# Head of a sort-attention and gated-MLP kernel: v loaded behind a memset, products of zeros between balancing steps, the first k sort in one-bank pieces

## The chip, the cores and the metric

One core of one Trainium2 chip. The metric is the device time of one execution in microseconds (us), as the median of several runs. Five engines work on it: TensorE (PE in the profile, its weight loads PEld), VectorE (DVE), ScalarE (ACT), GpSimd (POOL) and SyncE (SP); each runs its own list of instructions in order and waits on semaphores.

## What is computed

Attention over blocks whose keys and values are first mixed by a balanced matrix, then a two-layer network with the gate h cos h. Cut to what matters:

```
P = sort_net                                  # (4, 8, 8, 8)
for _ in range(5):                            # balancing
    P = exp(P - max(P)); P = P / (sum over columns + 1e-9); P = P / (sum over rows + 1e-9)
k_sorted = einsum('bhij,bhjcd->bhicd', P, k_blocks)     # 8 blocks of 96 rows, 64 wide
v_sorted = einsum('bhij,bhjcd->bhicd', P, v_blocks)
scores = q_block @ k_sorted_block.T / 8; attn = softmax(scores)
x = (attn @ v_sorted), reshaped to (3072, 512)
h = x @ w_in;  out = (h * cos(h)) @ w_out     # 512 -> 2048 -> 512
```

## The kernel before

The order on every engine is written out by hand. The work goes in eight units n (batch b = n // 2, half of the blocks), each with 4 block rows u. Per unit: `qk` (L368) makes scores of one block row in PSUM and subtracts the row maxima on DVE; `expo` (L379) takes the exponential on ACT; the result is turned by `p_transpose` (L392) on PE or by a DMA; `av` (L399) multiplies with v and divides on DVE; `x_transpose` (L428) turns the result into `xT`. `moe_up` (L477) then makes eight `h` tiles with cos on ACT and the product on DVE, and `moe_down` (L482) the output. Attention of unit n + 1 is put in slots between the pieces of `moe_up` and `moe_down` of unit n, so only the head, before the first `moe_up`, has attention alone.

The head, L141 to L529. POOL makes the identity, clears the padding of four `p_buf` tiles (L146), then issues the loads in this order: q of unit 0 (L148, instruction at L114), k of batch 0 in two halves (L149, L94), v of batch 0 in two halves (L150, L94), three quarters of `w_in` (L152, L135). Then it clears the rows of `vbuf` between v's halves (L154, L155), writes ones into `vS` (L159), and issues the last quarter of `w_in`, q of unit 1, `w_out`, k of batch 1 and q of unit 2 (L161 to L166). Later loads stand behind these in the same queue.

Meanwhile the balancing runs (L197 to L283), for two groups g of two batches each: one small product on PE (`sk`, L217) and a few DVE and ACT instructions per step. `keep_warm` (L179) puts products of a zero tile, 128x128 by 128x256, ahead of it (16) and behind its first two steps (6 and 6); nothing reads them. q of unit 0 is turned on PE in two of the steps (`q_turn`, L245). At the end `spread` (L233) writes the balanced matrix of each group into `bd` as a block diagonal.

`k_sort_b` (L284) applies it to k: for each column c of a block and each half of the heads, one product with 32 rows of `kbuf` as weights and 32 columns of `bd`. It takes 32 columns c per call, so a tile `ks` of two PSUM banks; the left half of the result is copied to `kT` by DVE, the right half by ACT (L291 to L298). Three calls make batch 0. `v_sort_b` (L325) does the same for v, eight products of 128x128 by 64 per call, copied by ACT to `vS`; eight such calls (`v_next`) stand between the first scores (L498 to L513).

PSUM has two pools: `big` (three buffers of two banks: `idle`, `ks`, `sc`, `av`, `h`) and `acc` (two buffers of one bank: `sk`, `vs`, `pps`, `xps`, `o`). A buffer is taken in turn, and its next writer waits for the readers of the last.

Of the kernel before, what the change touches and what calls it, by code (L numbers as in the profile page):

```python
# [10 lines left out]
FP32 = mybir.dt.float32  # L11
BF16 = mybir.dt.bfloat16
# [6 lines left out]
def kernel(  # L19
# [15 lines left out]
    nc = tc.nc  # L35
    B, H, S, D = q.shape
    nb = sort_net.shape[-1]
# [7 lines left out]
    H2 = H // 2  # L45
# [63 lines left out]
    def load_q(n):  # L109
        b, ih = n // 2, n % 2  # L110
        if n < NQ:

            t = qload.tile([blk, H, QR * D], BF16, name="qin", tag="qin")
            nc.gpsimd.dma_start(  # L114
                out=t[:], in_=q[b][:, ih * IC * blk:(ih + 1) * IC * blk].rearrange(
                    "h (p r) d -> p h (r d)", r=QR))
# [16 lines left out]
    def load_w_in(z):  # L133
        c = slice(z * Dff // 4, (z + 1) * Dff // 4)
        nc.gpsimd.dma_start(out=w_in_t[:, :, c], in_=w_in_d[:, :, c])  # L135
# [3 lines left out]
        nc.gpsimd.dma_start(out=w_out_t[:, c], in_=w_out_d[:, c])  # L139

    make_identity(nc, ident[:])  # L141
    NP = 4
    p_bufs = []
    for i in range(NP):
        t = const.tile([blk, 2 * H2, 128], BF16, name=f"p_buf{i}")
        nc.gpsimd.memset(t[:, :, blk:], 0.0)  # L146
        p_bufs.append(t)
    load_q(0)  # L148
    load(kbuf, kin_d, 0)  # L149
    load(vbuf, vin_d, 0)  # L150
    for z in range(3):
        load_w_in(z)  # L152

    nc.gpsimd.memset(vbuf[32:64, :CD], 0.0)  # L154
    nc.gpsimd.memset(vbuf[96:128, :CD], 0.0)  # L155
    VW = D + 2
    for g in range(NG):
        vS[g] = vsp.tile([blk, 4 * NB, VW], BF16, name="vS", tag="vS")
        nc.gpsimd.memset(vS[g][:, :, D:D + 1], 1.0)  # L159
        kT[g] = ktp.tile([128, 2 * NB, blk], BF16, name="kT", tag="kT")  # L160
    load_w_in(3)  # L161
    load_q(1)
    for z in range(4):
# [4 lines left out]
    order = const.tile([blk, blk], BF16, name="order")  # L168
    half_pi = const.tile([128, 1], FP32, name="half_pi")
    nc.vector.memset(half_pi[:], math.pi / 2)  # L170
    warm = const.tile([128, 256], BF16, name="warm")
    nc.vector.memset(warm[:], 0.0)
    nc.vector.memset(vbuf[:, CD:], 0.0)
    nc.vector.memset(vperm[:, CD:], 0.0)
# [3 lines left out]

    def keep_warm(times):  # L179

        idle = big.tile([128, 256], FP32, name="idle", tag="big")
        for _ in range(times):
            nc.tensor.matmul(idle[:], warm[:, :128], warm[:], start=True, stop=True)

    keep_warm(16)


    E = [const.tile([128, nb], FP32, name=f"E{g}") for g in range(NG)]
# [34 lines left out]
        nc.vector.scalar_tensor_tensor(  # L223
            L[g][:], rows_of, ci[g][:], along(E[g]), op0=ALU.mult, op1=ALU.mult)
    sk = [product(L[g], maskj) for g in range(NG)]
    keep_warm(6)
    nc.vector.tensor_copy(same[:], rows_of)
    for g in range(NG):
        nc.vector.tensor_scalar(
# [34 lines left out]
    for it in range(4):  # L264
        for g in range(NG):
            nc.scalar.activation(E[g][:], T[g][:], AF.Exp, scale=ci[g][:])
        if it > 1:
            copy_on(A, *turned)
        sk = [product(same, E[g]) for g in range(NG)]
        if it in (1, 2):  # L270
            turned = q_turn(0, it - 1, big, "big")
        elif it == 0:
            keep_warm(6)
        for g in range(NG):
            nc.vector.reciprocal(rr[g][:], sk[g][:])
            nc.vector.tensor_tensor_reduce(
                T[g][:], E[g][:], rr[g][:], 1.0, 1e-9, ALU.mult, ALU.add, cs[g][:])
            nc.vector.reciprocal(ci[g][:], cs[g][:])
            if it == 3:
                spread(g)  # L280

    def k_sort_b(b, c0, ncs, eng, pool, tag):

        ps = pool.tile([128, ncs, NB], FP32, name="ks", tag=tag)  # L284
        for t in range(ncs):
            c = c0 + t
            for hp in range(2):
                r = hp * 64 + b * 32
                x = hp * H + b * H2
                nc.tensor.matmul(  # L290
                    ps[hp * D:(hp + 1) * D, t], kbuf[r:r + 32, c * D:(c + 1) * D],  # L291
                    bds[0][r:r + 32, x:x + H2].rearrange("p x i -> p (x i)"),
                    start=True, stop=True)
        engs = eng if isinstance(eng, list) else [eng]
        w = NB // len(engs)
        for z, e in enumerate(engs):
            copy_on(e, kT[0][:, b * NB + z * w:b * NB + (z + 1) * w, c0:c0 + ncs],
                    ps[:, :, z * w:(z + 1) * w].rearrange("p t m -> p m t"))  # L298

    def k_sort_g(c0, ncs, eng, pool, tag):  # L300
        ps = pool.tile([128, ncs, 2 * NB], FP32, name="ks", tag=tag)
# [48 lines left out]
    def qk_part(n, u, part, pool, tag):  # L350
        g, b2, ih = where(n)
        w = len(part)
        sc = pool.tile([128, w, 512], FP32, name="sc", tag=tag)
        for e, hp in enumerate(part):
            for h2 in range(H2):
                m = (b2 * H2 + h2) * nb + ih * IC + u
                nc.tensor.matmul(  # L357
                    sc[:blk, e, h2 * blk:(h2 + 1) * blk],
                    qT[n][hp * D:(hp + 1) * D, u * H2 + h2, :],
                    kT[g][hp * D:(hp + 1) * D, m, :], start=True, stop=True)  # L360
# [126 lines left out]
    B, C = (big, "big"), (acc, "acc")  # L487


    vz = iter(range(16))  # L490

    def v_next(eng=A):
        z = next(vz)
        v_sort_b(z // 8, z % 8 * 8, 8, eng, *C)
# [9 lines left out]
    expo(0, 0, True)  # L504
    qk(0, 2)
    v_next()
    p_transpose(0, 0, A, *C)
    v_next()
    expo(0, 1, True)
    qk(0, 3)  # L510
    v_next()
    v_next()
    p_transpose(0, 1, V, *C)  # L513
# [18 lines left out]
    expo(1, 0, True)  # L532
    expo(1, 1, True)
    moe_down(0, [[(qk, 1, 2), (p_transpose, 1, 0, A, *B)],
                 [(k_sort_b, 1, 0, 32, [V, A], *B), (p_transpose, 1, 1, A, *B), (qk, 1, 3),
                  (expo, 1, 2, True)],
                 [(av, 1, 0, True), (av, 1, 1, True), (expo, 1, 3, True),
                  (p_transpose, 1, 2, A, *B)],
                 [(k_sort_b, 1, 32, 32, [V, A], *B), (x_transpose, 1, 0, V, *B),
                  (av, 1, 2, True), (p_transpose, 1, 3, A, *B)],  # L540
                 [(k_sort_b, 1, 64, 32, [V, A], *B), (av, 1, 3, True),
                  (x_transpose, 1, 1, V, *B)],
                 [(q_transpose, 2, 0, A, *B), (x_transpose, 1, 2, V, *B),
                  (x_transpose, 1, 3, V, *B)]])
# [119 lines left out]
```

## Time and profile before

| what | us |
|---|---|
| runs: median (lowest to highest of 3) | 276.68 (275.47 to 276.81) |
| profiled execution, whole | 278.54 |
| profiled execution, span | 276.8 |
| PE busy in the span | 249.6 (90%) |
| DVE, ACT, POOL busy | 171.0, 158.6, 95.4 |
| k of batch 0: issue begins, first k product | 3.24, 15.21 |
| bd of group 0 written | 12.98 |
| first score product, first up product | 23.49, 36.77 |

The page gives busy times by engine, the span in 40 slices of 6.92 us with PE's granted clock and the DMA engines' share, the chain of work that ended last, the costliest groups of instructions, and the DMA issues. Besides the page, the trace answers with the chain in order of time, busy times in chosen stretches, and the DMA queues in a stretch. A busy PE isn't PE at its peak: matmul ends are modelled, and at half clock the same product is longer.

### The profile page before, as it was taken

Reading aid. Unit: us, or ns where it says so; the run is one execution under the profiler, and the core shown is the slowest. Engines: PE = TensorE matmul, PEld = TensorE weight load, DVE = VectorE, ACT = ScalarE, POOL = GpSimd, SP = SyncE. Lnnn points to the kernel's source line nnn. Section 1 sums busy time; section 2 is a strip of 40 time slices with the busy share of each in tenths; the row PEclk is TensorE's granted clock in tenths of the full one; section 3 lists DMA queues with packets and bytes.
Section 4 is the critical chain, followed back from the end, with each engine's and each line's share of the span. In section 5 each row is a group of like instructions: output and inputs, shape, how many; then the busy total and the mean of one; then the engine's idle time right before and its main releaser. Section 6 shows DMA issues by size and latency. Waiting matters only on the chain.

```text
span 276.8 us, 6148 instructions
## 1 busy us (share of the span) xinstructions
PE 249.6 (90%) x2572; PEld 155.6 (56%) x2572; DVE 171.0 (62%) x308; ACT 158.6 (57%) x218; POOL 95.4 (34%) x118
## 2 busy tenths in 40 slices
PE   7659988999998899999999899998999699979994
PEld 5558877856565465555566455554555345535541
DVE  5625857976447653776338786788489618953710
ACT  3413935666486874769578854664557336635621
POOL 9996100999956977920004000001000000010000
PEclk9855559999999999999999999999999889999999
DMA  5999998907999993283649055207711930071012
GB/s 62 199 192 204 206 217 165 59 2 118 142 130 115 124 154 92 50 57 73 122 92 63 0 133 131 52 2 153 119 57 30 163 81 0 14 177 55 2 39 76
DMA packets 61100, 27.13 MB, mean 98 GB/s; under 512 B 48848, under 2 KB 58320, under 8 KB 60816
## 3 DMA queue, kind: packets, MB, share of 16 engines
q0 software_dynamic: 31040, 16.01, 41.5%
q1 hardware_dynamic: 29888, 10.72, 19.4%
q8 instruction: 20, 0.33, 0.5%
q14 instruction: 8, 0.07, 0.1%
q10 hardware_dynamic: 144, 0.00, 0.0%
HBM read 27.27 MB, written 6.29 MB: 121 GB/s over the span
## 4 chain that ended last, share of the span: by engine, by line
PE 73%; DVE 10%; DMA 9%; ACT 3%; issue 2%; POOL 1%; SPq 0%; POOLq 0%; ACTq 0%
PE h L446 30%; PE o L463 25%; DMA pT<-p_buf 4%; DMA kbuf<-in_k_dram 4%; PE sc L357 4%; PE ks L290 3%; PE av L409 2%; PE vs L328 2%; DVE mx L363 2%; PE pps L396 2%; DVE s L364 2%; DVE xn L418 2%; ACT c L450 2%; DVE gg L453 2%; DVE xT L241 2%
## 5 line engine op out<-in xcount | busy, mean ns | idle before, releaser
L446 PE MATMUL h<-xT,w_in_t 128*128 128x384 bf16 (+1 forms) x576 | 93.4, 313 | 4.5 <-DVE xT L241 4.0
L463 PE MATMUL o<-w_out_t,gg 128*128 128x512 bf16 x384 | 91.6, 384 | 2.9 <-DVE s L364 2.9
L453 DVE TENSOR_TENSOR gg<-c,h 128x768 bf16<-128x768 f32 (+1 forms) x72 | 62.0, 863 | 36.9 <-ACT c L450 35.6
L450 ACT ACTIVATE c<-h,half_pi 128x768 f32<-128x768 f32 (+1 forms) x72 | 59.8, 831 | 35.9 <-PE h L446 34.5
L446 PEld LDWEIGHTS <-w_in_t 128*128 128x128 bf16 x576 | 53.3, 100 | 31.8 <-issue 5.4
L463 PEld LDWEIGHTS <-gg 128*128 128x128 bf16 x384 | 35.4, 99 | 40.9 <-DVE s L364 3.5
L471 POOL DMA_DIRECT2D out_dram<-o_s x9 | 5.0, 552 | 98.6 <-ACT o_s L469 98.6
L363 DVE TENSOR_REDUCE mx<-sc 96x4 f32<-96x384 f32 (+1 forms) x43 | 32.0, 744 | 10.2 <-PE sc L357 10.0
L469 ACT COPY o_s<-o 128x512 f32<-128x512 f32 x24 | 14.1, 586 | 41.8 <-PE o L463 38.5
L364 DVE TENSOR_TENSOR s<-sc,mx 96x384 f32<-96x384 f32 (+1 forms) x43 | 32.2, 749 | 2.0
L121 POOL DMA_DIRECT2D qin<-in_q_dram x20 | 15.5, 781 | 46.9 <-DMA qT<-qin 30.3
L382 ACT ACTIVATE p_buf<-s 96x768 bf16<-96x768 f32 x32 | 26.5, 843 | 8.4 <-DVE s L364 7.9
L317 POOL COPY vperm<-vbuf 128x1536 bf16<-128x1536 bf16 x8 | 22.4, 2848 | 3.2 <-DMA vbuf<-in_v_dram 3.2
L418 DVE TENSOR_TENSOR xn<-av,r 96x512 bf16<-96x512 f32 x32 | 22.0, 687 | 1.3 <-DVE r L416 0.2
L239 ACT CAST vS<-vs 96x512 bf16<-96x512 f32 (+1 forms) x28 | 18.1, 648 | 5.2 <-PE vs L336 3.1
L239 ACT CAST kT<-ks 128x512 bf16<-128x512 f32 x18 | 10.3, 580 | 15.1 <-DVE kT L241 15.1
L409 PE MATMUL av<-vS,pT 96*128 96x65 bf16 (+1 forms) x256 | 13.5, 201 | 5.9 <-DMA pT<-p_buf 5.0
L409 PEld LDWEIGHTS <-pT 96*128 96x128 bf16 (+1 forms) x256 | 12.3, 105 | 11.1 <-DMA pT<-p_buf 5.8
L357 PE MATMUL sc<-kT,qT 64*96 64x96 bf16 x256 | 17.5, 223 | 1.1 <-DVE s L364 0.9
L357 PEld LDWEIGHTS <-qT 64*96 64x96 bf16 x256 | 11.9, 127 | 10.9 <-issue 8.6
L416 DVE RECIPROCAL r<-av 96x8 f32<-96x8 f32 x32 | 6.4, 200 | 16.5 <-PE av L409 16.2
L99 POOL DMA_DIRECT2D kbuf<-in_k_dram x24 | 13.3, 599 | 0.8 <-PE ks L290 0.8
(72 smaller groups left out, 204.2 us busy)
## 6 DMA issues: line engine op xcount, KB each, us to landing
out_dram<-o_s SPq DMA_DIRECT2D x15, 256.0 KB, 3.6
out_dram<-o_s POOLq DMA_DIRECT2D x9, 256.0 KB, 3.1
w_in_t<-in_moe_w_in_dram POOLq DMA_DIRECT2D x4, 512.0 KB, 14.1
w_out_t<-in_moe_w_out_dram POOLq DMA_DIRECT2D x4, 512.0 KB, 13.0
qin<-in_q_dram POOLq DMA_DIRECT2D x20, 96.0 KB, 3.6
kbuf<-in_k_dram POOLq DMA_DIRECT2D x4, 384.0 KB, 16.8
vbuf<-in_v_dram POOLq DMA_DIRECT2D x4, 384.0 KB, 13.3
kbuf<-in_k_dram POOLq DMA_DIRECT2D x24, 64.0 KB, 3.6
```

What stands on the lines that cost most here:

```text
L239: eng.copy(dst, src)
L317: nc.gpsimd.tensor_copy(vperm[:, :CD].rearrange("p (d c) -> p d c", d=D)[:, z * 16:(z + 1) * 16], vv[:, z * 16:(z + 1) * 16, :blk])
L357: nc.tensor.matmul(sc[:blk, e, h2 * blk:(h2 + 1) * blk], qT[n][hp * D:(hp + 1) * D, u * H2 + h2, :], kT[g][hp * D:(hp + 1) * D, m, :], sta ...
L363: nc.vector.reduce_max(mx[:], scv, axis=AX.X)
L364: nc.vector.tensor_tensor(s_t[n, u][:, part[0]:part[0] + w], scv, mx.to_broadcast([blk, w, H2, blk]), op=ALU.subtract)
L382: nc.scalar.activation(p[:, :, :blk], s_t.pop((n, u)).rearrange("p e h c -> p (e h) c"), AF.Exp, scale=scale)
L409: nc.tensor.matmul(a[:w, hp, h2 * (D + 1):(h2 + 1) * (D + 1)], pt[:blk, e * blk:e * blk + w], vS[g][:, v_at(g, b2, hp, h2, ih * IC + u), : ...
L418: nc.vector.tensor_tensor(xn.rearrange("p h e d -> p e h d"), avv[:, :, :, :D], r.to_broadcast([blk, 2, H2, D]), op=ALU.mult)
L446: nc.tensor.matmul(h[:, f2, :w], w_in_t[:, kk, f * 128:(f + 1) * 128], xT[n][:, kk, lo:hi], start=(kk == 0), stop=(kk == KC - 1))
L450: nc.scalar.activation(c[:, :, :w], h[:, :, :w], AF.Sin, bias=half_pi[:, 0:1])
L453: nc.vector.tensor_tensor(gt[n, fp][:, :, lo:hi], c[:, :, :w], h[:, :, :w], op=ALU.mult)
L463: nc.tensor.matmul(o[:], gt[n, f // 2][:, f % 2, ts * 128:(ts + 1) * 128], w_out_t[:, f, :], start=(f == 0), stop=(f == FC - 1))
```

## The change

Five things, all but the last in the head:

1. POOL issues q and k directly behind the identity; the `p_buf` memsets come after them. v is issued behind the memset of the rows 32 to 63 of `vbuf`. The two memsets of `vbuf` write the same bytes as half as many 4-byte elements; the second comes behind the `w_in` issues.
2. The product of zeros is 128x128 by 128x512, its moving operand one column read again and again. There are 8 ahead of the balancing, 3 behind its first step, and 3, 1, 1, 4 behind the next four (before: 16, 6, and 6 behind the first of these).
3. `k_sort_b` takes 16 columns per call, one bank, and one engine copies the whole piece. Batch 0 goes as six pieces, alternating `big` with DVE and `acc` with ACT; batch 1, in `moe_down(0)`, as six pieces in `big`, alternating DVE and ACT.
4. `kT` of group 0 is laid out in groups of 16 columns, so that a copy writes one contiguous run; the score products read their moving operand in six pieces of 16.
5. In the head, `qk(0, 2)` and `qk(0, 3)` come earlier against `expo` and `p_transpose`, as the diff shows.

```diff
-    NP = 4
+    load_q(0)
+    load(kbuf, kin_d, 0)
+    NP = 4
     ...
         nc.gpsimd.memset(t[:, :, blk:], 0.0)
-    load_q(0)
-    load(kbuf, kin_d, 0)
+    nc.gpsimd.memset(vbuf[32:64, :CD].bitcast(FP32), 0.0)
     load(vbuf, vin_d, 0)
     for z in range(3):
         load_w_in(z)
-    nc.gpsimd.memset(vbuf[32:64, :CD], 0.0)
-    nc.gpsimd.memset(vbuf[96:128, :CD], 0.0)
+    nc.gpsimd.memset(vbuf[96:128, :CD].bitcast(FP32), 0.0)
...
+    KG = 16
+    kT0 = kT[0].rearrange("p n c -> p (n c)").rearrange(
+        "p (b z m c) -> p b z m c", b=2, z=blk // KG, c=KG)
...
-    warm = const.tile([128, 256], BF16, name="warm")
+    warm = const.tile([128, 128], BF16, name="warm")
...
-        idle = big.tile([128, 256], FP32, name="idle", tag="big")
+        idle = big.tile([128, 512], FP32, name="idle", tag="big")
-            nc.tensor.matmul(idle[:], warm[:, :128], warm[:], start=True, stop=True)
+            nc.tensor.matmul(
+                idle[:], warm[:], warm[:, :1].to_broadcast([128, 512]), start=True, stop=True)
-    keep_warm(16)
+    keep_warm(8)
...
-    keep_warm(6)
+    keep_warm(3)
...
-        elif it == 0:
-            keep_warm(6)
+        keep_warm((3, 1, 1, 4)[it])
...
-    def k_sort_b(b, c0, ncs, eng, pool, tag):
-        ps = pool.tile([128, ncs, NB], FP32, name="ks", tag=tag)
-        for t in range(ncs):
+    def k_sort_b(b, c0, eng, pool, tag):
+        ps = pool.tile([128, KG, NB], FP32, name="ks", tag=tag)
+        for t in range(KG):
     ...
-        engs = eng if isinstance(eng, list) else [eng]
-        w = NB // len(engs)
-        for z, e in enumerate(engs):
-            copy_on(e, kT[0][:, b * NB + z * w:b * NB + (z + 1) * w, c0:c0 + ncs],
-                    ps[:, :, z * w:(z + 1) * w].rearrange("p t m -> p m t"))
+        copy_on(eng, kT0[:, b, c0 // KG], ps.rearrange("p t m -> p m t"))
...
-                m = (b2 * H2 + h2) * nb + ih * IC + u
+                m = h2 * nb + ih * IC + u
+                rows = slice(hp * D, (hp + 1) * D)
+                keys = kT0[rows, b2, :, m] if g == 0 else kT[g][rows, b2 * NB + m]
...
-        k_sort_b(0, z * 32, 32, [V, A], *B)
+        k_sort_b(0, z * 2 * KG, V, *B)
+        k_sort_b(0, (z * 2 + 1) * KG, A, *C)
     v_next()
     qk(0, 0)
     v_next()
     qk(0, 1)
     v_next()
     v_next()
+    qk(0, 2)
+    v_next()
     expo(0, 0, True)
-    qk(0, 2)
-    v_next()
+    v_next()
+    qk(0, 3)
+    expo(0, 1, True)
     p_transpose(0, 0, A, *C)
-    v_next()
-    expo(0, 1, True)
-    qk(0, 3)
     v_next()
     v_next()
     p_transpose(0, 1, V, *C)
...
-                 [(k_sort_b, 1, 0, 32, [V, A], *B), (p_transpose, 1, 1, A, *B), (qk, 1, 3),
+                 [(k_sort_b, 1, 0, V, *B), (k_sort_b, 1, 16, A, *B), (p_transpose, 1, 1, A, *B), (qk, 1, 3),
```

The other two calls for batch 1 are split in the same way.

More of the change, by code (lines that the diff above doesn't have):

```diff
@@ L355, in qk_part @@
             for h2 in range(H2):
-                m = (b2 * H2 + h2) * nb + ih * IC + u
+                m = h2 * nb + ih * IC + u
+                rows = slice(hp * D, (hp + 1) * D)
+                keys = kT0[rows, b2, :, m] if g == 0 else kT[g][rows, b2 * NB + m]
                 nc.tensor.matmul(
                     sc[:blk, e, h2 * blk:(h2 + 1) * blk],
-                    qT[n][hp * D:(hp + 1) * D, u * H2 + h2, :],
-                    kT[g][hp * D:(hp + 1) * D, m, :], start=True, stop=True)
+                    qT[n][rows, u * H2 + h2, :], keys, start=True, stop=True)
         scv = sc[:blk, :, :H2 * blk].rearrange("p e (h c) -> p e h c", c=blk)
@@ L487 @@
     B, C = (big, "big"), (acc, "acc")
-    vz = iter(range(16))
+    vz = iter(range(0, 128, 8))
     def v_next(eng=A):
         z = next(vz)
-        v_sort_b(z // 8, z % 8 * 8, 8, eng, *C)
+        v_sort_b(z // D, z % D, 8, eng, *C)
     for z in range(3):
-        k_sort_b(0, z * 32, 32, [V, A], *B)
+        k_sort_b(0, z * 2 * KG, V, *B)
+        k_sort_b(0, (z * 2 + 1) * KG, A, *C)
     v_next()
@@ L503 @@
     v_next()
-    expo(0, 0, True)
     qk(0, 2)
     v_next()
+    expo(0, 0, True)
+    v_next()
+    qk(0, 3)
+    expo(0, 1, True)
     p_transpose(0, 0, A, *C)
-    v_next()
-    expo(0, 1, True)
-    qk(0, 3)
     v_next()
@@ L538 @@
                   (p_transpose, 1, 2, A, *B)],
-                 [(k_sort_b, 1, 32, 32, [V, A], *B), (x_transpose, 1, 0, V, *B),
+                 [(k_sort_b, 1, 32, V, *B), (k_sort_b, 1, 48, A, *B), (x_transpose, 1, 0, V, *B),
                   (av, 1, 2, True), (p_transpose, 1, 3, A, *B)],
-                 [(k_sort_b, 1, 64, 32, [V, A], *B), (av, 1, 3, True),
+                 [(k_sort_b, 1, 64, V, *B), (k_sort_b, 1, 80, A, *B), (av, 1, 3, True),
                   (x_transpose, 1, 1, V, *B)],
```

## The prediction

> **What bounds the kernel now.** I read the page first, for the clock row and the chain, then the chain in order of time for the first 40 us, then busy time by stretch, then the DMA view. All times are from the one profiled execution: span 276.8 us, 278.54 us in all. The median of the runs shown is 276.68, so I work out a difference against the profiled execution and put it on the median.
>
> The page has PE busy for 90% of the span, so whatever delays PE early is paid at the end. Its clock row shows where PE is slow; each digit is 6.92 us:
>
> ```profile
> PEclk9855559999999999999999999999999889999999
> ```
>
> From about 11.5 to 42 us TensorE has half its clock. The chain in order of time (start, length, what) shows the same stretch:
>
> ```profile
> 1.33 1.01 POOL p_buf L146 x4
> 2.33 0.90 POOL qin L114
> 3.24 11.93 DMA kbuf<-in_k_dram
> ...
> 15.21 4.14 PE ks L290 x142
> 19.35 1.84 issue
> 21.19 1.53 PE ks L290 x28
> ...
> 24.11 0.56 PE sc L357 x6
> ```
>
> The head is a chain of four p_buf memsets on POOL, the q issue, the k transfer, the k sort, a hole of 1.84 us in it, the scores. The balancing of the sort matrix is not on it: the timeline has bd for group 0 written by 12.98, while k lands at 15.21. The hole carries no wait, only "issue". The DMA view from 18 to 20 us shows what lies there:
>
> ```profile
> q0 software_dynamic: 399, 0.40, 121.6%
> q8 instruction: 1, 0.02, 2.8%
> ```
>
> One instruction block is fetched while the data queue is full. The page has 20 such packets for about 5,140 PE instructions, so some 257 each. In the trace the 142nd k product is near row 461 of PE's stream, the block before it was entered near 15.8, and PE goes on at 21.19: 5.4 us from entering a block to having the next, against 3.6 us in which PE ran 256 short instructions.
>
> The last view is busy time by stretch, with stretches cut at the clock's steps. The steps in the trace stand at 4.67, 11.50, 42.22, 219.71 and 223.13 us: distances of 2, 9, 52 and 1 times 3.413. So the clock is decided every 3.41 us. Columns: stretch, length, busy (count) of PE, PEld, DVE, ACT, POOL, then the clock in it:
>
> ```profile
> 4.67:8.09 3.42, 2.69 (x21) 2.05 (x20) 2.44 (x19) 0.95 (x4) 3.38 (x6) 1.00 1.38 178
> 8.09:11.50 3.41, 2.68 (x42) 2.19 (x42) 2.16 (x19) 1.89 (x6) 3.41 (x1) 1.00 0.97 191
> 14.91:18.33 3.42, 3.12 (x111) 3.07 (x113) 0.69 (x1) 0.30 (x1) 3.42 (x1) 0.50 1.16 194
> 38.81:42.22 3.41, 3.41 (x32) 3.23 (x30) 2.04 (x4) 0.73 (x3) 0.00 (x0) 0.50 1.23 238
> 216.30:219.71 3.41, 0.85 (x11) 0.30 (x9) 1.91 (x2) 1.04 (x2) 0.54 (x1) 1.00 1.24 164
> ```
>
> The first two are equally busy; the first (12 products of zeros, 128x128) keeps the clock, the second (32 small transposes) loses it. The third is almost full of k products of 32 rows by 64 columns and does not win the clock; the fourth, full of 128x128 work, does. So busy time does not decide, but how much of the array the products use. Weighted by rows and columns, the shapes give 0.38, 0.15, 0.11, 0.85 and 0.10 for the five: it rises somewhere between 0.64 (the stretch 35.39 to 38.81, not risen) and 0.85, and falls somewhere between 0.15 and 0.33 (the lowest that kept it, 66.1 to 69.5).
>
> **Part by part.**
> *q and k issued ahead of the p_buf memsets.* 1.01 us leave the chain ahead of k: -1.0. The packets recorded for k and v are 12,288 bytes at 926 ns, eight one after another on each of four DMA engines per issue, 7.4 us; k and v end together at 15.0 to 16.2 on different engines. **v behind a memset therefore takes nothing off k**, except that k packets took up to 1.2 us between 8 and 10.5: 0 to -0.4; I take 0. k lands near 14.2, behind bd (12.98).
>
> *The memsets.* Half as many elements of twice the width: POOL's 6144 elements took 5.21 us, so 2.6 if elements count, 5.2 if bytes do. I take 2.6 (the p_buf row, 303 ns for 256, also goes by elements). v is then issued at 7.1 instead of 4.42 and lands near 17; at the other end near 20. First use is at about 21, so both hide. Behind it on POOL, w_in moves from 5.55 to 8.2, and its fourth quarter from 19.27 to some 14.5; first use of w_in is past 35. If that cover failed, each us late would be a us.
>
> *Products of zeros.* 8, 3, 3 of 512 columns replace 16, 6, 6 of 256: the same columns. New are 1, 1 and 4. At full clock a 512-column product is 0.21 us (two of 256 took 0.27 in the second batch), so each of the two single ones delays the next balancing step by about 0.2, at half clock 0.4: bd at 13.4 to 13.8, still ahead of k. The four fill PE to about 13. Cost 0; without the cover of k's transfer +0.4 to +0.8.
>
> *k sort in six pieces.* The 192 products stay. With k at 14.2, the half clock and the same 5.4 us for the block, they end 7.4 after k (before 7.5), so -1.0 to -1.1. If the added products hold the clock until 18.33, the block is entered 0.3 earlier: -1.4. I take **-1.2**. The second copy no longer waits for the first (DVE 0.69, then ACT 0.59), but PE has eight v products meanwhile: what it waited was 0.22, **-0.2**. That sc now reads its moving operand in six pieces of 16 is in no row; the nearest, vs (two pieces of 32), takes 0.41 for eight against 0.29 for its weight loads: at most 0.12 for each of 16 score tiles, +1.9, and nothing below 0, as the columns are the same; I take 0, since it is the weight load that paces vs in the long run (0.34). In the later moe_down the same split lets DVE copy half a tile earlier; PE waited 0.54 there for xT (68.7 to 69.3) behind that copy: **-0.4**, bounds 0 and -0.6.
>
> *Other order.* qk(0,3) goes ahead, which closes 0.74 us of DVE idle (30.4 to 31.1), off PE's path. The copy of the first pT on ACT now stands behind exp(0,1) (0.85) and a v product waits for that PSUM buffer: **+0.5**, bounds 0 and +0.85.
>
> *The clock.* The added products lift 8.09 to 11.50 from 0.15 to about 0.28, between the bounds: it may hold. But k sort then runs 2 us and PE waits some 3 us for instructions, a stretch of 0.03 to 0.11, under a value that fell (0.15). So **I expect half clock again by 18.33 or 21.74**, and full clock as soon as a stretch is full of up products; these start 1.2 us earlier, and the boundary at 38.81 may now do. Each us more at full clock saves about half: 0 to -1.1, I take **-0.5**.
>
> [...]
>
> **Sum:** -1.2 -0.2 +0.5 -0.5 -0.4 = -1.8 us. Profiled 276.7; on the median **274.9 us**. Behind the head PE is the bound, so a shift carries through to the end.
>
> **Rivals.**
> 1. *The clock holds.* For it: 0.28 in the stretch that fell. Against: k sort as above. From 24.6 to 42.2 PE was above 90% busy; at full clock eight v products are 0.34 instead of 0.86, eight transposes 0.50 instead of 0.88, eight up products 0.66 instead of 1.28, and ACT (eight vS copies 0.59, two exps 0.85, pT 0.8: 7.2) becomes the bound. Over this stretch that is 7.1 to 4.4 us less. In all -5.5 to -7.5: 269 to 271; in part, if it falls later, 271 to 273. Chance 0.18.
> 2. *Nothing to see.* The first q packet comes no earlier (its transfer crawls until 5.0, beside P_a's), so k lands at 15 as before, or the order costs its 0.85: 0 to -1.3, 275.4 to 276.7. Chance 0.22.
> 3. *Slower: the instruction block waits behind v.* Entered at about 14.9, its fetch now meets v's 926 ns packets, moved to 9 to 17 us, where before it met w_in packets of 98 ns. If it lies on an engine of v, up to five packets are ahead: +1.5 to +4.6 on the k sort. It decides when the 5.4 us become more than 7.2; over 8.6 it is slower by more than 0.5%. 276.7 to 279.5. Chance 0.12 over 0.5%, 0.05 under it.
>
> The forecast (273 to 275.4) has 0.43. A measurement of this kernel tells about 0.5% from no change, 1.4 us. Faster by more (under 275.3): 0.38 of the forecast, all of rival 1 and a bit of rival 2: 0.57. Slower: rival 3, 0.12, and 0.02 for w_in or the kT reads: 0.14. The rest, 0.29, is the same. Range 270.0 to 278.0: most of rival 1, the lower part of rival 3.
>
> **What would show it.** Right: first k product near 14.2, "issue" of 1.5 to 3.2 us within the k sort, clock at half by 21.74, first up product (before 36.77) near 35.5. Wrong: first k product at 15 (rival 2), clock still full at 25 us (rival 1), a hole over 4 us in the k sort, with the q8 packet late in it (rival 3).

## The result and the profile after

The changed kernel takes 277.99 us (median of 20 runs, 277.15 to 278.81) against 276.7 us for the kernel before (20 runs of the same kernel, 275.47 to 280.14). The ratio is 1.0038, interval 1.0019 to 1.0056: slower by 0.4%, where 1.8 us less had been forecast. The profiled execution of after takes 277.17 us, with a span of 275.4; the one of before took 278.54. So the two profiles stand the other way round from the medians, and have to be read stage by stage:

| us | before | after |
|---|---|---|
| second group's sort matrices in use (`nmx`) | 3.97 | 6.17 |
| first balancing product | 5.27 | 7.98 |
| bd of group 0 begun | 12.63 | 16.27 |
| k of batch 0 landed, its two halves | 15.17, 15.34 | 14.21, 14.61 |
| first k product | 15.21 | 17.96 |
| first score product | 23.49 | 25.91 |
| first up product | 36.77 | 39.09 |
| second `moe_up` begins | 76.42 | 77.81 |
| sixth `moe_down` | 208.40 to 225.52 | 210.04 to 224.03 |

k lands 0.7 to 1.0 us sooner, about as forecast, and PE takes it up 2.75 us later. The loss is 2.3 us at the first up product and 1.4 to 1.6 from the second `moe_up` up to 208 us. At the sixth `moe_down` the profiled run of before then loses 3.1 us that after does not lose. That the 1.4 is near the 1.3 of the medians says little: the profiled run of after, 277.17, is the second lowest of its 20, and 17 of them, with mean granted clocks of 0.932 or 0.999 to 1.000 against its 0.943, lie 0.3 to 1.6 us above it; no trace shows one of these.

The clock row of after, in slices of 6.89 us:

```profile
PEclk9765558999999999999999999999999999999999
```

The half clock lasts into the seventh slice again, to 42.85 us (before 42.22). The dip of before near the 32nd slice is missing. The chain of after in order of time (start, length, what) answers to the one shown of before:

```profile
1.99 4.17 DMA P_a<-in_sort_net_dram
...
6.81 0.71 DVE order L211
...
8.45 0.39 PE sk L222 x2
8.83 1.29 PE idle L187 x3
10.13 0.65 PE sk L222 x4
10.78 1.29 PE idle L187 x3
...
16.54 1.49 PE idle L187 x3
18.02 4.11 PE ks L294 x75
22.13 1.70 issue
23.83 1.30 PE ks L294 x42
...
25.98 0.50 PE sc L359 x8
```

POOL and the k transfer are gone from it. The head is now bound by the other branch: the load of the sort matrices, a DVE copy of 0.71 (0.22 in before), the balancing with products of zeros between its steps and behind it, and then the k sort with a hole of 1.70 us (1.84 in before). bd is written at 16.62, and the last four products of zeros hold the first k product until 17.96. Three things in this chain were not in the forecast, and each is tried below.

The sort matrices: from 4.0 to 6.5 us the DMA view of after has two queues, with packets, MB and the time of the packets as a share of 16 engines' time (it can pass 100%):

```profile
q0 software_dynamic: 902, 0.46, 132.0%
q10 hardware_dynamic: 72, 0.00, 3.9%
```

In the same stretch of before only the first of them has packets:

```profile
q0 software_dynamic: 599, 0.31, 114.1%
```

q10 is the second load on ScalarE's queue, 64 packets of 32 bytes and 8 of 4. In before its packets ran from 3.40 to 3.61, ahead of q's, whose first came at 3.96. With q issued at 1.54 instead of 2.29, q's packets of 512 bytes begin at 3.22, and those of q10 run from 4.72 to 5.81 among them.

The clock: busy time by stretch of after, columns as in the prediction:

```profile
5.30:8.71 3.41, 0.65 (x5) 0.56 (x6) 2.40 (x12) 0.39 (x2) 3.41 (x4) 1.00 0.84 140
8.71:12.13 3.42, 3.42 (x14) 2.08 (x13) 1.43 (x12) 1.19 (x4) 3.38 (x4) 0.50 0.98 151
12.13:15.54 3.41, 3.02 (x43) 2.29 (x43) 2.00 (x17) 1.77 (x6) 3.36 (x5) 1.00 1.00 190
15.54:18.95 3.41, 3.01 (x43) 1.85 (x46) 1.75 (x10) 0.81 (x2) 1.56 (x3) 0.50 1.07 192
```

With the late start PE was busy for 0.65 of the 3.41 us before 8.71, the clock on record went to 0.50 at 8.71, and six products of zeros of 512 columns ran in that stretch: 1.29 us for three.

### The profile page after: what moved, and what is told of

Read it like the earlier page. It is cut to its first block, busy times and chain, and to the rows that moved or that the text cites. A ratio compares the mean times of both kernels' runs of the same rounds, so it can differ in the third digit from the quotient of the medians.

```text
span 275.4 us, 6110 instructions
## 1 busy us (share of the span) xinstructions
PE 248.3 (90%) x2543; PEld 153.6 (56%) x2564; DVE 171.6 (62%) x308; ACT 158.5 (58%) x218; POOL 90.2 (33%) x118
## 4 chain that ended last, share of the span: by engine, by line
PE 75%; DVE 11%; DMA 6%; ACT 4%; issue 2%; SPq 1%; ACTq 0%; DVEq 0%
PE h L447 30%; PE o L464 24%; DMA pT<-p_buf 4%; PE sc L359 4%; PE ks L294 3%; PE av L410 3%; DVE mx L364 2%; PE vs L328 2%; DVE s L365 2%; PE pps L397 2%; DVE xn L419 2%; ACT c L451 2%; PE idle L187 2%; DVE gg L454 2%; DMA P_a<-in_sort_net_dram 2%
## 5 line engine op out<-in xcount | busy, mean ns | idle before, releaser
L464 PE MATMUL o<-w_out_t,gg 128*128 128x512 bf16 x364 | 86.9, 379 | 4.2 <-DVE s L365 2.9
L447 PEld LDWEIGHTS <-w_in_t 128*128 128x128 bf16 x576 | 52.7, 99 | 31.9 <-issue 5.5
L470 ACT COPY o_s<-o 128x512 f32<-128x512 f32 x24 | 14.1, 586 | 39.8 <-PE o L464 36.4
L359 PE MATMUL sc<-kT,qT 64*96 64x96 bf16 x256 | 17.1, 223 | 0.9 <-DVE s L365 0.9
L410 PE MATMUL av<-vS,pT 96*128 96x65 bf16 (+1 forms) x256 | 13.1, 198 | 4.7 <-DMA pT<-p_buf 3.8
## 6 DMA issues: line engine op xcount, KB each, us to landing
kbuf<-in_k_dram POOLq DMA_DIRECT2D x4, 384.0 KB, 14.2
vbuf<-in_v_dram POOLq DMA_DIRECT2D x4, 384.0 KB, 13.1
```

Source lines behind the costliest of these rows:

```text
L359: nc.tensor.matmul(sc[:blk, e, h2 * blk:(h2 + 1) * blk], qT[n][rows, u * H2 + h2, :], keys, start=True, stop=True)
L410: nc.tensor.matmul(a[:w, hp, h2 * (D + 1):(h2 + 1) * (D + 1)], pt[:blk, e * blk:e * blk + w], vS[g][:, v_at(g, b2, hp, h2, ih * IC + u), : ...
L447: nc.tensor.matmul(h[:, f2, :w], w_in_t[:, kk, f * 128:(f + 1) * 128], xT[n][:, kk, lo:hi], start=(kk == 0), stop=(kk == KC - 1))
L464: nc.tensor.matmul(o[:], gt[n, f // 2][:, f % 2, ts * 128:(ts + 1) * 128], w_out_t[:, f, :], start=(f == 0), stop=(f == FC - 1))
```

## The experiments

Every kernel was timed beside the kernel before on the same chip; the ratio is to those runs (their medians: 278.0 us for e1 to e12, 278.3 for e14 to e18, 277.75 for e20 to e24). Traces are compared by stage, since the totals also hold what happens at 217 us (the fourth part below).

The clock has to be read with care. In eight of the traces (e1, e2, e10, e12, e14, e16, e20, e21) the first step of the clock on record comes between 40.0 and 43.8 us, and the page's clock row reads full from the start. But their products of zeros take 0.59 to 0.63 us (512 columns) or 0.37 to 0.42 (256 columns) to the last, as long as in half-clock stretches of after and e3, where at full clock e4 has 0.38 and before 0.27. From these lengths I take it that the head of these eight ran at half clock, which is what "from the start" and "throughout" mean below.

### The late sort matrices and the copy beside a memset

`e1_q_behind_pbuf`, after with the old place of q and k:

```diff
-    load_q(0)
-    load(kbuf, kin_d, 0)
     NP = 4
     ...
+    load_q(0)
+    load(kbuf, kin_d, 0)
     nc.gpsimd.memset(vbuf[32:64, :CD].bitcast(FP32), 0.0)
```

> The changed kernel with one part undone: the p_buf memsets stand ahead of the q and k issues again. Theory A (the earlier q issue puts q's packets in front of the second sort-matrix load of the ACT queue, so the balancing starts 2.2 us late): that load lands near 4.0 instead of 6.15, bd of group 0 is written by 13.5 instead of 16.6, the first k product is near 15.3 instead of 18.0, the first up product near 37 instead of 39.1, and the time falls by 1.5 to 2.5 us against the changed kernel, to 275.5 to 276.5. Theory B (the products of zeros between the balancing steps and ahead of the k sort cost the time): the load lands at 4.0 but the first k product stays at 16.5 or later, and the time stays at 277.3 or more.

Measured 277.55 us, ratio 0.9994 (0.9959 to 1.0029). The sort matrices landed at 3.9 again, and the first k product came at 18.30, later than in after (which had full clock in two stretches of the head). The late load alone does not explain the loss. DVE's timeline of this kernel (start, length, engine, line) shows what took its place:

```profile
3.88 0.16 DVE L203 TENSOR_REDUCE nmx<-P_a 128x1 f32<-128x8 f32 x1 [0.51 <-DMA P_a<-in_sort_net_dram]
...
4.43 2.75 DVE L211 COPY order<-ident 96x96 bf16<-96x96 bf16 x1
4.58 2.61 DVE L227 RECIPROCAL ci<-cs 128x1 f32<-128x1 f32 x1
7.24 0.35 DVE L228 SCALAR_TENSOR_TENSOR L<-maskh,ci,E 128x128 f32<-128x128 f32 x1
```

The copy took 0.22 us in before. It now begins beside the first `vbuf` memset, which the change moved from 7.91 to 4.47 on POOL, and ends 0.06 us behind it (7.18 and 7.12). The reciprocal behind it on DVE is shown as 2.61 long, up to the copy's end; the next one, behind no copy, takes 0.16. In after both delays are there and overlap: the late load brings the copy to 6.73, when the memset has 0.7 us left. Taking away one uncovers the other.

`e3_q_first_alone`, before with q and k ahead of the `p_buf` memsets, nothing else:

> The kernel before with one part done: q and k are issued ahead of the p_buf memsets. Theory A: the sort-matrix load lands near 6.1, bd near 15.5 (its 12.98 plus 2.2 and some 0.3 for the slower DVE), the first k product follows it instead of k at 14.2, so 0.3 to 1.0 us slower than before, near 277.3. Theory B: the load has slack, the first k product is near 14.3 and the kernel is about 1 us faster than before, near 275.7.

Measured 279.7 us, ratio 1.0079 (1.0042 to 1.0116). The load landed at 5.99, bd began at 16.37, and the first k product came at 16.87 (before 15.21), though k was there at 14.7.

`e8_v_memset_alone`, before with v behind the 4-byte memset, nothing else:

> The kernel before with one part of the change: v's load is issued behind the first of the two clearings of vbuf, which are written as fp32, so that the first clearing starts near 4.5 us instead of 7.9. q and k stay behind the four p_buf clearings. Theory C (a clearing on POOL holds up VectorE's 96x96 bf16 copy of the order matrix and the reciprocal behind it): the sort matrices land at 3.9 as before, yet the copy lasts 2 to 3 us in place of 0.22, the first balancing product comes at 7.2 to 7.7 in place of 5.3, bd at 15 to 16.4 in place of 12.6, the first k product near 15.6 to 16.7; the time is 0.3 to 1.4 us over that of before (ratio 1.001 to 1.005). Theory A alone (only the late sort-matrix load counts): copy 0.22, first balancing product 5.3, first k product 15.2, ratio 1.000.

Measured 279.95 us, ratio 1.0080 (1.0042 to 1.0119). The copy took 2.69 us, the first k product came at 16.60. Either move alone costs 1.4 to 1.7 us at the first k product, and 1.7 (e3) or 1.8 (e8) at the first up product.

`e10_no_head_reorder`, after with both moves undone (q, k and v as in before, both `vbuf` memsets as bf16 behind the `w_in` issues):

> The kernel after with both moves in POOL's queue undone: p_buf clearings ahead of q and k, v ahead of both vbuf clearings, as bf16. The zeros between the steps, the k sort in pieces and the new unit order stay. If the two moves together are the whole loss (A and C, each hiding the other), the sort matrices land at 3.9, the order copy lasts 0.22, bd comes at 12.9 to 13.2, the first k product at 15.0 to 15.3, the first MoE up product at 35.5 to 36.7 (39.1 in after), and the time falls 1.5 to 3 us under that of after, ratio to before 0.990 to 0.997. If the zeros (theory B), the pieces or the order lose the time instead, the first MoE up product stays at 38 to 39 and the ratio at 1.000 or above.

Measured 274.91 us, ratio 0.9924 (0.9893 to 0.9956); copy 0.22, first k product at 15.84, first up product at 37.10, second `moe_up` at 75.72 against 77.81 in after. So the two moves in POOL's queue are the whole loss, and more. bd came at 14.55, later than the 12.9 to 13.2 expected.

`e11_order_copy_late`, e1 with the copy of the order matrix moved behind the last balancing step:

```diff
-    nc.vector.tensor_copy(
-        order.rearrange(...), ident[...].rearrange(...))
     rows_of = maskh.to_broadcast([128, 2 * H, nb])
 ...
         turned = q_turn(0, it - 1, big, "big")
 ...
                 spread(g)
+    nc.vector.tensor_copy(
+        order.rearrange(...), ident[...].rearrange(...))
```

> The kernel after with p_buf clearings ahead of q and k again (so the sort matrices land at 3.9) and with VectorE's copy of the order matrix moved behind the last balancing step; the vbuf clearing stays at 4.5 us on POOL. Theory C (the copy is what the clearing holds up, and the reciprocal only stands behind it): the ci reciprocals last 0.15 beside the clearing, the first balancing product comes at 5.0 to 5.5, bd at 12.6 to 13.4, the first k product near 15.2, ratio 0.990 to 0.998. If the clearing slows every VectorE operation, whatever stands first: the reciprocal itself lasts 2 to 2.7, the first balancing product stays at 7.3 to 7.7, ratio 0.998 to 1.002.

Measured 276.44 us, ratio 0.9965 (0.9932 to 0.9999). Neither case as written: the reciprocals took 0.16 and the first balancing product came at 5.06, but bd began at 15.24. DVE's timeline shows why:

```profile
5.38 1.81 DVE L229 COPY same<-maskh 128x128 f32<-128x128 f32 x1
5.52 1.67 DVE L231 TENSOR_SCALAR_CACHE_REDUCE T<-sk 128x8 f32<-128x8 f32 x1
5.60 1.59 DVE L231 DVE_READ_ACCUMULATOR T<-sk 128x1 f32 x1
```

The next copy, an fp32 one, met the rest of the memset and took 1.81 us (0.22 in before). So it is not the copy of the order matrix alone: of the two copies of the head, the one that met the memset was long.

`e14_copies_on_ScalarE`, e1 with both copies on ACT:

```diff
-    nc.vector.tensor_copy(
+    nc.scalar.copy(
         order.rearrange(...), ident[...].rearrange(...))
...
-    nc.vector.tensor_copy(same[:], rows_of)
+    nc.scalar.copy(same[:], rows_of)
```

> The kernel after with the p_buf clearings ahead of q and k again, and with both copies of the head, of the order matrix and of the row mask (same), done by ScalarE instead of VectorE; the vbuf clearing stays at 4.5 us on POOL. Refined theory C (a clearing on POOL holds up a copy on VectorE, whichever copy comes, and what stands behind it; the other VectorE operations run beside it): no VectorE operation of the balancing lasts over 0.5 us, the first balancing product comes at 5.0 to 5.4, bd at 12.7 to 14.7, the first k product at 15.1 to 16.0, the first MoE up product at 36.3 to 37.3, ratio 0.989 to 0.996. If the clearing holds up other operations too, the next of them lasts 1.5 us or more, bd comes at 15.2 or later and the ratio stays at 0.996 or above.

Measured 275.15 us, ratio 0.9897 (0.9860 to 0.9934). ACT's timeline and DVE's, with the memset still running from 4.5 to 7.1:

```profile
4.61 0.34 ACT L211 COPY order<-ident 96x96 bf16<-96x96 bf16 x1
4.85 0.29 ACT L232 COPY same<-maskh 128x128 f32<-128x128 f32 x1
```

```profile
5.19 0.35 DVE L228 SCALAR_TENSOR_TENSOR L<-maskh,ci,E 128x128 f32<-128x128 f32 x1
5.76 0.17 DVE L234 TENSOR_SCALAR_CACHE_REDUCE T<-sk 128x8 f32<-128x8 f32 x1 [0.23 <-PE sk L222]
```

The other DVE operations in this stretch kept their lengths of before: reciprocals 0.15 to 0.16, reductions 0.17, scalar-tensor-tensor operations 0.35. The head is that of e10: first k product at 15.79, first up product at 37.04. So of what DVE does there, only copies, and what stood behind them, were long beside the memset: 2.75 (e1), 2.69 (e8), 1.81 (e11). In e1 the copy's record begins at 4.43, 0.04 us ahead of the memset's, and yet the copy lasts until the memset's end. How the memset holds a copy up is not shown.

`e12_both_causes_gone`, after (q and k first) with the second group's sort matrices on SyncE's queue alone and the order copy late as in e11:

> The kernel after, with everything it reorders kept, and two things moved out of the way: the second group's sort matrices are loaded from the sync engine's queue alone instead of half from ScalarE's, and the copy of the order matrix stands behind the last balancing step. If theory A is about the queue of ScalarE, the sort matrices land by 4.5, the first balancing product comes at 5.0 to 5.8, bd at 12.5 to 13.5, and the first k product follows k's landing, 14.2 to 14.7; first MoE up product 34.8 to 36; time 1 to 2.5 us under that of before (ratio 0.990 to 0.996). If q's packets delay a small load in any queue, the sort matrices still land at 5.5 to 6.2, the first balancing product at 6.8 to 7.3, bd at 15 to 16, the first k product at 16 to 16.5, and the ratio is 0.996 to 1.002.

Measured 277.64 us, ratio 1.0023 (0.9993 to 1.0053). The idea failed: the load landed at 6.96, later than on two queues (6.17). So the delay doesn't belong to ScalarE's queue; with q issued first, this small load was late on either (3.97 in before).

`e24_q_first_other_causes_gone`, after with both copies on ACT and the zeros as (3, 0, 0, 0), q and k still first:

> The kernel after with q and k still ahead of the p_buf clearings, so that k lands at 14.2 to 14.6 and the second group's sort matrices at 5.9 to 6.2, but with both copies of the head on ScalarE and no zeros behind the second to fourth balancing step. Theory A as a trade: the balancing starts at 7.0 to 7.4 and ends with bd at 14.2 to 15.4 when the clock is full or half; the first k product comes at 14.9 to 15.8, so that k's earlier landing is worth 0.3 us at most, and first MoE up product at 36.0 to 37.0; ratio 0.988 to 0.995. If the earlier landing is worth the 1.0 us of the prediction once the other causes are gone: first k product 14.2 to 14.6, first MoE up product 35.2 to 35.8, ratio under 0.988.

Measured 275.70 us, ratio 0.9951 (0.9917 to 0.9986). Its chain:

```profile
1.99 3.94 DMA P_a<-in_sort_net_dram
5.96 0.16 DVE nmx L203
...
16.18 0.35 DVE bd L239
...
16.67 4.34 PE ks L295 x156
```

k lay there from 14.6, and its first product came at 16.67: the earlier k is worth nothing, since the same move makes the balancing late. Both cases of the expectation were too good, as the balancing again ran at half clock, from 7.49 on.

### The products of zeros

`e2_no_added_zeros`, after with

```diff
-        keep_warm((3, 1, 1, 4)[it])
+        if it == 0:
+            keep_warm(3)
```

> The changed kernel without the added products of zeros behind the second, third and fourth steps (1, 1 and 4 of 512 columns); 8, 3 and 3 stay. Theory A: the sort-matrix load still lands at 6.1, bd is at 15.8 to 16.6, the first k product follows at once (before: 1.3 us behind bd, where the four products at half clock ended), so 1.0 to 1.6 us are gained: 276.4 to 277.0. Theory B: bd comes back by over 1 us as well and the time falls by 2 us or more, under 276.

Measured 277.18 us, ratio 0.9999 (0.9967 to 1.0031); first k product at 17.57, 0.4 before after's, at a clock that was half throughout.

`e4_zeros_alone`, before with the new zeros (8, 3 and 3, 1, 1, 4 of 512 columns), nothing else:

> The kernel before with one part done: the products of zeros of the change (8, 3, 3, 1, 1, 4 of 512 columns). Theory A: bd at 13.3 to 13.6, still ahead of k at 15.2, so within 0.3 us of before, or faster if the clock holds longer. Theory B: the first k product is pushed to 16 or later and the kernel is over 1 us slower than before, near 278.

Measured 275.2 us, ratio 0.9918 (0.9884 to 0.9953). In the head nothing changes: bd ends at 12.99, the first k product comes at 15.10, the first up product at 36.62. The gain of 0.8% has to come from elsewhere (the fourth part).

`e17_order_and_pieces`, e10 with the zeros as (3, 0, 0, 0):

> The kernel after without both moves in POOL's queue and without the zeros behind the second to fourth balancing step (3, 0, 0, 0): what is left of the change is the k sort in pieces, the other unit order, and fewer but wider zeros ahead of the balancing. Theory B (zeros between steps cost when the clock is at half): bd comes at 12.6 to 13.6 whatever the clock does, the first k product at 15.0 to 15.3 with k's landing, the first MoE up product at 36.2 to 36.8, 0.3 to 0.9 us ahead of the kernel that keeps these zeros (37.1), ratio 0.986 to 0.993. If zeros between the steps are free here too: first k product 15.8, first MoE up product 37.1, ratio 0.992.

Measured 275.14 us, ratio 0.9912 (0.9876 to 0.9948): first k product at 15.27, first up product at 36.43. The time is that of e10 within the intervals. The profiled run of e10 had half clock from the start and this one only from 11.71, so 37.10 against 36.43 mixes zeros and clock. A cleaner pair is e10 with e16 (below), which has the old zeros and half clock from the start too: bd began at 14.55 and 14.32, the first k product came at 15.84 and 15.33. So the added zeros cost 0.5 us at half clock and nothing at full clock (e4). And half clock alone moves bd from 12.6 to 14.3: "whatever the clock does" in the expectation was wrong.

### The k sort in pieces and the order

`e20_pieces_alone`, before with the first zeros as in e16 and the k sort in pieces of 16 columns:

> The kernel before with the first 16 zeros written as 8 (as in e16_first_zeros_half_as_many, so that the tail stall is out of the comparison) and the k sort in one-bank pieces of 16 channels, each copied by one engine; nothing else. The prediction's terms: k product to first MoE up product 1.4 us shorter than the 21.5 to 22.0 of kernels without pieces, that is 20.1 to 20.6. The joint measure of pieces and order so far (21.2 to 21.3 with both): if the order costs what was predicted (0.5), pieces give 20.7 to 20.9; if the order costs nothing, 21.1 to 21.5. The hole inside the k sort stays at 1.5 to 2.0 us, if the instruction block and not the copies sets it. Ratio 0.986 to 0.992.

Measured 274.34 us, ratio 0.9892 (0.9853 to 0.9931), the lowest time of the study. By the ratio it is no better than e16 (0.9903) within the intervals; the trace shows the gain. First k product to first up product took 21.02 us, against 21.56 in before and 21.83 in e16. The 1.4 of the expectation counted in the earlier landing of k, which this stretch can't hold. Its chain at the k sort:

```profile
15.38 4.17 PE ks L297 x149
19.56 1.78 issue
21.34 1.30 PE ks L297 x23
22.64 0.84 PE vs L331 x8
23.49 0.50 PE sc L362 x8
```

The hole is about as long as before (1.84). From first k product to first score took 8.34 us, in before 8.28, in e16 8.57: the k sort gained 0.2 at most. The gain comes behind it, 12.68 instead of 13.28 us from there to the first up product. In e16 the last six of the first eight scores waited for ACT's half of the copy, which stood behind DVE's half (0.70, then 0.59); DVE began the row maxima of the first scores 1.21 us after the first score product. In e20 it began them after 0.62.

`e21_order_alone`, the same with the new unit order in place of the pieces:

> As e20_pieces_alone, with the new unit order in place of the pieces. The prediction's term: k product to first MoE up product 0.5 us longer than 21.5 to 22.0, that is 22.0 to 22.5; if the order costs nothing 21.5 to 22.0; if it gains, under 21.4. Ratio 0.988 to 0.994.

Measured 275.92 us, ratio 0.9947 (0.9917 to 0.9977). k product to first up product took 22.30 us: the order costs 0.5 to 0.7, as forecast.

### Eight instructions and a stall 200 us later

`e16_first_zeros_half_as_many`: before, with the first 16 zeros written as 8 of twice the width:

```diff
-    keep_warm(16)
+    idle = big.tile([128, 512], FP32, name="idle", tag="big")
+    for _ in range(8):
+        nc.tensor.matmul(idle[:], warm[:, :128], warm[:, :1].to_broadcast([128, 512]), ...)
```

> The kernel before with the first 16 products of zeros of 256 columns written as 8 of 512, the same TensorE time from 8 instructions fewer; nothing else is changed. Theory D (8 instructions fewer on TensorE move its 16 KB instruction-block packet, which in before lies at 217.5 us among the DMA transposes of pT and holds them up): the head stays as in before within 0.3 us (first k product 15.0 to 15.4), the packet lies at 219 to 223, the stretch of the sixth MoE down lasts 13.5 to 14.5 in place of 17.1, no run lies above 277.6, ratio 0.988 to 0.996. If the tail stall has another cause, the ratio is 0.998 to 1.002 and runs over 278 are about half.

Measured 275.17 us, ratio 0.9903 (0.9864 to 0.9941); its 6 runs lie from 274.58 to 275.40. Of the 22 runs of before on that chip, 12 were 278.3 or more and the other ten 275.7 to 276.9. The head gained nothing (first up product at 37.16).

`e18_eight_more_instructions`, e10 with 8 one-column products added behind the first zeros:

```diff
     keep_warm(8)
+    tiny = big.tile([128, 512], FP32, name="tiny", tag="big")
+    for _ in range(8):
+        nc.tensor.matmul(tiny[:, :1], warm[:], warm[:, :1], start=True, stop=True)
```

> The kernel after without both moves in POOL's queue (as e10_no_head_reorder), with 8 one-column products of zeros added behind the first group, so that TensorE has as many instructions as in before. They last some 0.1 us each, beside the wait for the sort matrices. Theory D: the head stays as in e10 (first MoE up product 36.8 to 37.4), the instruction-block packet goes back to 215.5 to 218.5, among the DMA transposes of pT, and the time rises by 1 to 3.5 us over that of e10 in most runs, ratio to before 0.995 to 1.003. If the tail stall has another cause, nothing changes: ratio 0.990 to 0.995.

Measured 277.72 us, ratio 0.9982 (0.9946 to 1.0018); 7 of its 12 runs were 277.6 or more, the other five 275.7 to 276.3. By the ratios that is 1.6 us over e10, by the medians, from two chips, 2.8, with a head no later than e10's (first up product at 36.83). So eight instructions of TensorE decide this, at 217 us. The DMA queues from 217 to 219 us, first of before, then of e16, then of e18:

```profile
q1 hardware_dynamic: 1059, 0.26, 149.6%
q8 instruction: 1, 0.02, 3.1%
```

```profile
q1 hardware_dynamic: 1130, 0.28, 77.9%
```

```profile
q1 hardware_dynamic: 713, 0.17, 131.3%
q8 instruction: 1, 0.02, 3.1%
```

q1 carries the DMA transposes of `pT` and `xT`. q8 has 20 packets of 16,384 bytes in before, which I take for instruction blocks of TensorE, since their places move with the number of its instructions (below). In before and e18, with such a packet among the transposes (at 217.46 and 217.05), q1's packets take 149.6 and 131.3% of the engines' time and end late; in e16 more of them take 77.9%. In the chain, before, e16 and e18:

```profile
214.87 4.84 DMA pT<-p_buf
219.70 0.05 issue
219.75 0.64 PE av L409 x8
```

```profile
214.35 3.55 DMA pT<-p_buf
```

```profile
214.45 4.85 DMA pT<-p_buf
```

PE waits for `pT`, and in before the clock falls to half at 219.71 for 3.41 us on top of that. With fewer instructions ahead, the packet lies at 219.8 (e16) or 222.3 (after and e4), when these transposes are done. All kernels with 28 products of zeros (before, e3, e8, e18) have it between 217 and 219 and need 15.3 to 17.1 us for the sixth `moe_down`; all those with 20 or fewer need 13.1 to 14.1. Shown are the place of the packet, the length of the transposes and the change of both by eight instructions; what inside the DMA engines holds the transposes up is open.

Why about half of before's runs escape the larger loss can be estimated from the clock. PE waits for `pT` about equally long in all four kernels with the packet there: 2.60 us in before, 2.57 in e18, 2.37 in e3, 2.71 in e8 (1.15 in e16). In the traces of before and after the steps on record stand whole multiples of 3.41 us apart (2, 9, 52, 1 and 16; 1, 1, 1, 8 and 68), so I count stretches of 3.41 us on from the first step of each trace. In before and e18 nearly the whole wait lies in one such stretch, with PE busy 0.85 (the row in the prediction) and 1.26, and the clock was at half behind it. In e3, and likewise in e8, a boundary counted in this way cuts the wait in two, PE is busy 2.29 and 2.16, and the clock stayed at 1.00 (columns as in the prediction, e3):

```profile
215.66:219.07 3.41, 2.29 (x24) 1.02 (x20) 2.13 (x5) 1.43 (x2) 0.53 (x1) 1.00 1.30 192
219.07:222.48 3.41, 2.16 (x22) 1.22 (x23) 1.84 (x3) 0.85 (x1) 0.02 (x1) 1.00 0.45 129
```

The first step on record stands at another place in these traces: 4.67 in before, 4.03 in e3, 5.30 in after. The mean granted clocks of the runs of before on e16's chip fit: the ten lower runs have 0.950 or 0.997 to 1.000, the twelve upper ones 0.938 or 0.992, and one stretch of 3.41 us at half takes 0.006 from the mean over 276.8 us. So I estimate the late transposes at about 1.3 us (e16's median against the middle of the ten) and the fall of the clock, where it comes, at about 2 more. That all of before's lower runs have the packet among the transposes is not shown, since only one run of each kernel has a trace.

## Why the prediction was wrong

- *"The balancing of the sort matrix is not on it: bd ... written by 12.98, while k lands at 15.21", and q and k ahead worth -1.0: the step that failed.* k landed at 14.2 as computed. But bd, the other condition of the first k product, was kept at its time of before, though two of its inputs depend on what was moved: its load runs among q's packets (4.72 to 5.81 instead of 3.40 to 3.61), and its copy lasts until the end of POOL's memset (0.71 in after, 2.75 in e1, 0.22 in before). The first alone costs 1.5 to 1.7 us at the first k product (e24, e3), the second alone 1.4 (e8), both together 2.75, with the zeros at half clock in it. The slack of 2.2 us was also read at full clock: from the first balancing product to bd, before takes 7.36 us, and e16, at half clock from the start, 9.06, so that its bd is written 0.6 ahead of k's landing (14.67 and 15.28). After the late start the clock was at half where before had full (0.50 from 8.71, behind the row 5.30:8.71; in e3 from 7.45). It is not the clock alone: against e16's first k product at 15.33, e3 is still 1.5 later and e24 1.3. Rival 2 even named the stretch in which q's transfer "crawls until 5.0, beside P_a's", but looked only at q's side of it.
- *Memsets, 2.6 us each, "hidden".* Their length was right (2.65). v's later landing (18.3 and 19.5) was hidden. What was missed is what runs beside a memset that starts at 4.80 instead of 7.91: the copy, 2.75 in e1. The sum needs what runs on the other engines as well as the queue.
- *Zeros, cost 0, without cover 0.4 to 0.8.* Both ends were met: 0 in e4, 0.5 at half clock. In after the cover was gone; without the added ones (e2) the first k product comes 0.4 earlier. Nor did they hold the clock: it fell at 11.24 in e4, at 11.50 in before.
- *k sort -1.2, copies -0.2.* Of the -1.2, about 1.0 is k's earlier landing, the failed step; 0.4 is left for what the pieces do from the first k product on, and e20 shows 0.5 (against before) to 0.8 (against e16). The k sort itself gained 0.2 at most, and its hole stayed (1.70 in after, 1.78 in e20). The 5.4 us from entering a block were an estimate from counted rows; the traces show the packet (from 18.81 in before, 21.48 in after) and PE going on at 21.19 and 23.83. The copies were under-sized: priced at PE's wait of 0.22, they let DVE begin the first row maxima 0.6 us earlier, which the first up product sees in full.
- *Order +0.5.* Right: 0.5 to 0.7 (e21). The kT reads cost nothing that shows.
- *Batch 1, -0.4.* In the `moe_down` that holds it, e20 stands 0.86 us ahead of e16 at the start, and 1.12 at the `moe_up` behind it: -0.26.
- *Clock, "half clock again by 18.33 or 21.74".* Right: half by 15.54. The gain of 0.5 did not come, since up products came later. But the clock gave some of the loss back: it rose at 42.22 in before and at 42.85 in after, so from the first up product on 5.45 us ran at half clock in before and 3.76 in after, and 2.3 us became 1.4. The bounds of array use are estimates from the rows of before; no run was made to try them.
- *Not in the sum:* the stall at 217 us, which eight instructions fewer avoid: about 1.3 us, and 2 more in runs of before whose clock falls there. The prediction saw that stall in before (the stretch 216.30:219.71) and the 20 block packets, and did not join them. e3 and e8, each with one of the two moves and without this gain, are slower by 0.8%.

The rivals: the slower one named the wrong mechanism (the block behind v's packets; the hole was 1.70). The best version found keeps only the pieces and the fewer instructions (e20, 0.9892; e14 and e16, at 0.9897 and 0.9903, are the same within the intervals).

## What to carry to other kernels

Where two branches meet (here k and bd), moving work for one needs the other branch walked again, through everything the moved work now runs beside: the DMA engines in that stretch (a load 2.2 us later here), and what the other engines run there (a copy of 2.75 us instead of 0.22). A slack of 2 us was no proof here against a small load that came to run beside a large one. When two causes overlap, undoing one shows nothing; undo both, then each alone.

## What was not expected of the hardware

- A copy on VectorE (96x96 bf16 in e1, 128x128 fp32 in e11) that met a GpSimd memset of 2.65 us lasted until the memset's end: 2.75 and 1.81 us instead of 0.22. Reciprocals (0.15 to 0.16), reductions (0.17) and scalar-tensor-tensor operations (0.35) beside it kept their length (e14).
- A load of 72 packets of at most 32 bytes landed 2.2 us later (6.17 instead of 3.97, after and before) when a load with 512-byte packets was issued on another queue 0.75 us sooner (at 1.54 instead of 2.29), and 3.0 us later (6.96, e12) when it stood third in SyncE's queue.
- With an instruction-block packet among them the DMA transposes ahead of the wait at 217 us took 4.8 to 5.1 us (before, e3, e8, e18), in the other kernels 3.0 to 3.7; eight instructions 200 us earlier moved the packet there (e18) or away (e16).
- A wait of TensorE of 2.4 to 2.7 us there was followed by a clock of 0.50 for 3.41 us in before, and by half clock in e18, where the wait lay in one stretch; in e3 and e8, where by the count of stretches a boundary cut it, the clock stayed at 1.00.
